# Layer B with token-major keys and heads innermost, query features of three chunks held at once, masks in halves, and the first loads reordered: a scheduled two-layer attention kernel

## The chip, the cores and the metric

The kernel runs on one core of one Trainium2 chip. The metric is device time in microseconds (us) of that core for one execution. The kernel before took 632.72 us (median of 3 runs, 631.79 to 635.19). Five engines matter: PE (matrix multiplies; PEld is its weight load, which overlaps it), ACT (activation functions, copies), DVE (vector work), POOL (masks, small work) and SP (issues transfers). Runs come with a state, fast or slow. Every comparison below is between fast runs.

## The reference, cut to what matters

Two different attention layers, A and B, alternate, twice: A, B, A, B, each with a layer norm ahead and a residual sum. There are 2048 tokens, 512 features, 32 heads of 16.

```python
def _A_ref(x, wq, wk, wv, wo, beta):      # causal softmax inside 4 segments of 512 tokens, plus a
    ...                                   # memory M, z carried from one segment to the next
        logits = einsum('bhqd,bhkd->bhqk', qs, ks) * scale + mask
        a_dot = einsum('bhqk,bhkd->bhqd', softmax(logits), vs)
        a_mem = (pq @ M) / (pq @ z + 1e-06)
        o = g * a_mem + (1.0 - g) * a_dot
        M = M + einsum('bhld,bhle->bhde', phi(ks), vs)
    ...
def _B_ref(x, wqkv, w_phi, wo):           # linear attention over all 2048 tokens
    ...
    phi_k = concatenate([softmax(pk), softmax(-pk)])   # pk = k @ w_phi, softmax over a head's 16
    kv = einsum('bhsf,bhsd->bhfd', phi_k, v)           # needs the keys of every token
    z = einsum('bhsf->bhf', phi_k)
    num = einsum('bhqf,bhfd->bhqd', phi_q, kv)
    den = einsum('bhqf,bhf->bhq', phi_q, z)[..., None] + 1e-06
    return (num / den) ... @ wo
```

One thing shapes the whole time line: a query of B needs `kv` and `z`, sums over all tokens. B's keys and values can follow A segment by segment, but no query product of B can start before A's last segment has passed through B's keys. Each layer pair therefore ends in a stretch of query work alone; after the second pair, nothing else is left to run beside it.

## The kernel before

The program is a graph of operations. A list scheduler with estimated durations orders them on each engine at build time, giving each operation its tiles from pools; a class of tiles may have a cap on how many are alive.

```python
LAT = {"pe": 190, "act": 160, "dve": 130, "pool": 100, "sp": 60}
...
                while ready[e]:                       # forward(): the pick on each engine
                    pr, i = heapq.heappop(ready[e])
                    o = ops[i]
                    if o.eng is not None:
                        continue
                    if can_alloc(o):                  # a free tile, and the class under its cap
                        pick = o
                        break
                    skipped.append((pr, i))
...
        self.pD = Pool("pD", dbl, psum=True)          # 2 PSUM tiles D, 128x1024 f32
        self.pG = Pool("pG", sgl, psum=True)          # 4 PSUM tiles G, 128x512 f32
...
N_XT, N_Q4, N_K1, N_K2, N_VT, N_SM, N_KT = 5, 7, 28, 14, 5, 6, 6
CAP2 = {"EQ": 6, "ET": 4}      # EQ: a 128x1024 block of query features, 4 for each chunk of 512 tokens
TOK = {3: ((0, 1, 2), (3,))}   # only chunk 3 has token-major keys
```

A's attention makes scores (S) in a D tile, an exp of 1024 columns on ACT, and on the diagonal a mask on POOL:

```python
self.mm(... KT.t[:, hf, j * 128:(j + 1) * 128], Q4.t[:, :, i * 128:(i + 1) * 128] ..., opens=[PT], label="S")
self.act(lambda PT=PT: PT.t[:], lambda S=S: S.t[:], ACT.Exp, 1024, [S], [PT], scale=0.25, label="exp")
if j == i:
    v(lambda e, pt8=pt8: e.affine_select(pt8(), pt8(), [[0, 8], [1, 128]], ...), 1080, [PT], [PT], eng="pool", label="mask")
```

B's keys of chunks 0 to 2 are feature-major: logits in D tiles, exps of 1024 columns, normalisers by small matmuls (Zk), then DMA transposes to token-major for the KV product:

```python
def b_keys(self, L, c):
    for gp in range(2):
        S = self.T(self.pD, "S")                      # the same two D tiles as A's scores
        ... # 8 BK matmuls of 512 columns
        for sgn in range(2):
            self.act(... ACT.Exp, 1024, [S[0], S[512]], [ET[sgn]], scale=1.0 - 2.0 * sgn, label="kexp")
            self.mm(... [8] * 8, [ET[sgn], R("H8b")], [Zb[(gp, sgn)]], label="Zk")
            for gg in range(2):
                self.tr(... , label="Etr")            # DMA transpose
    ... # reciprocal of Zk, BV matmuls, values times reciprocal, KV matmuls
```

B's queries: 16 BQ matmuls a chunk, exps into EQ, normalisers Zq, a serial scaling on ACT and DVE, and then for each of 4 token tiles a product N, a multiply on DVE straight from PSUM, an output projection:

```python
def b_query(self, L, c, store):
    ...
        self.wproj(S, gg * 512, self.WB["q"], ..., opens=[EQ[(gp, 0)], EQ[(gp, 1)]], label="BQ")
        self.act(... ACT.Exp, 1024, [S[0], S[512]], [EQ[(gp, sgn)]], label="qexp")
    ... # Zq, then Ln, Exp, five small DVE steps, Ln, Exp
    for tt in range(4):
        N = self.T(self.pD, "S")
        ...
        v(lambda e, ...: e.tensor_tensor(Tm.t[:].rearrange("p (s h d) -> p s h d", s=2, h=H),
                                         N.t[:].rearrange("p (s h d) -> p s h d", s=2, h=H),
                                         ab()[:, tt, :, :, None].to_broadcast([128, 2, H, DH]), ALU.mult), 1131, ..., label="nmul")
```

The softmax here doesn't subtract the row's maximum and nothing guards it: scores larger than these inputs give would overflow.

## Time and profile before

The stretches are cut at A's scores: their first and last matmul in each of the two layer pairs. This is the view of busy time by window, kernel before. After the window and its length come the busy time of each engine in it (with instructions), the granted PE clock as a share of full, the DMA share and GB/s.

```profile
core 0: us, PE busy (x) PEld busy (x) DVE busy (x) ACT busy (x) POOL busy (x), PEclk, DMA share, GB/s
0.00:27.70 27.70, 9.64 (x40) 4.02 (x41) 22.86 (x56) 12.07 (x21) 19.18 (x33) 0.98 0.58 184
27.70:248.90 221.20, 202.33 (x2289) 114.00 (x2320) 172.24 (x348) 190.08 (x223) 94.04 (x121) 0.98 0.33 63
248.90:318.20 69.30, 55.52 (x511) 33.12 (x518) 48.31 (x103) 37.16 (x59) 8.33 (x19) 0.87 0.10 22
318.20:546.60 228.40, 207.31 (x2316) 115.26 (x2348) 171.59 (x344) 194.81 (x231) 87.91 (x109) 0.98 0.32 56
546.60:632.80 86.20, 60.58 (x534) 34.98 (x539) 46.27 (x84) 32.79 (x53) 1.88 (x3) 0.84 0.19 47
```

The five lines are start-up, scores of the first pair, the query work between, scores of the second pair, and the tail. In the score stretches PE is about 91% busy. In the tail PE has 61 of 86 us, DVE 46, ACT 33: no engine is full, and the clock has dropped to 0.84.

Three lines of the page, kernel before: busy time with its share of the span, and PE's busy share and granted clock in tenths over 40 equal slices.

```profile
PE 535.4 (85%) x5680; PEld 301.4 (48%) x5760; DVE 461.3 (73%) x932; ACT 466.9 (74%) x586; POOL 211.3 (33%) x285
...
PE   1688998999999898679898888999989999958775
...
PEclk9889999999999999859989899999989999976897
```

The row of the clock shows two dents, at the ends of the two score stretches: there PE was busy for only 5 to 8 tenths of a slice.

The waits, kernel before: what ACT waited for at L514 over the whole span (us in total, times, longest). L514 is the helper of all exps, so the line holds key and query exps too, and the longest wait, 8.1 us, is a query exp of the tail shown below. The same view for the two score stretches alone gives 22.7 and 24.1 us.

```profile
ACT p L514 <- PE D L508: 73.2, 92, 8.1
```

Groups of instructions by line and shape, kernel before: busy us and mean ns, then idle time before them and its causes. They are the query multiply, the layer norm's last step xn, and a bf16 add.

```profile
L1086 DVE TENSOR_TENSOR p<-D,pS 128x1024 bf16<-128x1024 f32 x32 | 38.0, 1215 | 1.9 <-PE D L508 1.7
...
L754 DVE TENSOR_SCALAR p<-X,mv,rstd 128x512 bf16<-128x512 bf16 x48 | 32.9, 688 | 16.0 <-POOL rstd L743 15.4
...
L782 DVE TENSOR_TENSOR p<-p 128x512 bf16<-128x512 bf16 x48 | 27.1, 567 | 0.3
```

Last, the timeline of the tail, kernel before, between two multiplies of L1086: start, busy us, engine, line, operation (count), and in brackets the idle time before it.

```profile
592.17 2.35 DVE L1086 TENSOR_TENSOR p<-D,pS 128x1024 bf16<-128x1024 f32 x2
...
593.85 4.80 PE L508 MATMUL D<-pX,WB_q 128*128 128x512 bf16 x15 [1.58 <-DVE p L1086]
...
596.96 2.99 ACT L514 ACTIVATE p<-D 128x1024 bf16<-128x1024 f32 x3 [8.09 <-PE D L508]
...
599.77 0.35 PE L508 MATMUL G<-Rz,p 128*128 128x16 bf16 x8
...
600.62 1.03 ACT L514 ACTIVATE p<-D 128x1024 bf16<-128x1024 f32 x1
...
603.27 0.64 ACT L514 ACTIVATE pS<-pS 128x128 f32<-128x128 f32 x2
...
604.27 2.35 DVE L1086 TENSOR_TENSOR p<-D,pS 128x1024 bf16<-128x1024 f32 x2
```

These lines follow one chunk change from top to bottom. PE projects the next chunk's queries (4.80 us), ACT makes the features, the last of them at 600.62 and 1.03 us long, Zq matmuls run, Ln and Exp scale, and only at 604.27 does the next multiply start. With a cap of 6 on EQ tiles and 4 to a chunk, the next chunk's last features can't be made before this chunk has given its own back.

### The profile page before, as it was taken

The page shows a single profiled execution, that of the slowest core. Times are in us where ns is not written, and L with a number is a line of the kernel's source. Part 1 is how long each engine was busy: PE and PEld are TensorE (multiplying, and loading weights), DVE is VectorE, ACT ScalarE, POOL GpSimd, SP SyncE. Part 2 cuts the span into 40 slices and gives each one's busy share as a digit, 9 for nine tenths or more (in the row PEclk, how much of TensorE's full clock was granted, in tenths as well). Part 3 has the DMA queues.
Part 4 walks back from the last instruction along what each step waited for, and adds up shares of the span by engine and source line. Part 5 has one row for each costly group of instructions (what it writes and reads, how often), then busy time and mean ns, then how long its engine had stood idle before and what let it go on. Part 6 is the DMA issues. An engine that isn't in the chain of part 4 may idle for free.

```text
span 632.8 us, 13820 instructions
## 1 busy us (share of the span) xinstructions
PE 535.4 (85%) x5680; PEld 301.4 (48%) x5760; DVE 461.3 (73%) x932; ACT 466.9 (74%) x586; POOL 211.3 (33%) x285
## 2 busy tenths in 40 slices
PE   1688998999999898679898888999989999958775
PEld 0344544555556455355444444456445555526342
DVE  8789888688686585567779847778948758755563
ACT  4468999899889898427768789898969889733442
POOL 8483426225335432002223435433523533200000
PEclk9889999999999999859989899999989999976897
DMA  3872423421241241000353222352133133001232
GB/s 100 267 137 63 78 52 51 82 46 40 54 75 21 43 76 19 2 1 8 75 88 79 55 35 66 60 77 44 43 62 65 19 52 67 11 0 34 60 84 75
DMA packets 110511, 37.38 MB, mean 59 GB/s; under 512 B 101584, under 2 KB 109296, under 8 KB 110448
## 3 DMA queue, kind: packets, MB, share of 16 engines
q1 hardware_dynamic: 109088, 31.75, 26.3%
q0 software_dynamic: 1360, 4.74, 2.3%
q8 instruction: 45, 0.74, 0.5%
q14 instruction: 18, 0.15, 0.1%
HBM read 6.32 MB, written 2.10 MB: 13 GB/s over the span
## 4 chain that ended last, share of the span: by engine, by line
PE 42%; DVE 34%; ACT 9%; POOL 6%; DMA 5%; issue 3%; SPq 0%; POOLq 0%
PE G L508 24%; PE D L508 16%; ACT p L514 7%; DVE p L1086 3%; DMA p<-p 3%; DVE stats L738 3%; DVE pK L522 3%; DVE p L754 3%; DVE p L782 3%; POOL rstd L743 2%; DVE X L933 2%; DVE p L776 2%; POOL p L873 1%; DVE p L893 1%; DVE p L522 1%
## 5 line engine op out<-in xcount | busy, mean ns | idle before, releaser
L514 ACT ACTIVATE p<-D 128x1024 bf16<-128x1024 f32 x376 | 366.9, 1030 | 75.6 <-PE D L508 73.2
L873 POOL TENSOR_SCALAR_AFFINE_SELECT p<-p 128x1024 bf16<-128x1024 bf16 x128 | 141.7, 1112 | 190.1 <-ACT p L514 189.3
L508 PE MATMUL D<-pQ,pK 128*128 128x512 bf16 x640 | 181.8, 382 | 13.6 <-ACT p L514 6.7
L508 PEld LDWEIGHTS G<-pV,p 128*128 128x128 bf16 x2656 | 85.1, 96 | 33.5 <-POOL p L873 8.1
L508 PE MATMUL G<-pV,p 128*128 128x17 bf16 (+1 forms) x2656 | 89.4, 173 | 6.3 <-POOL p L873 2.6
L508 PEld LDWEIGHTS D<-pQ,pK 128*128 128x128 bf16 x640 | 49.7, 97 | 71.3 <-ACT p L514 32.2
L741 POOL TENSOR_SCALAR rstd<-mv 128x1 f32<-128x1 f32 x64 | 15.6, 246 | 151.8 <-DVE mv L739 151.2
L933 DVE TENSOR_TENSOR X<-X,G 128x512 bf16<-128x512 bf16 x32 | 21.9, 684 | 35.4 <-PE G L508 35.3
L738 DVE BATCH_NORM_STATS2 stats<-X 128x6 f32<-128x512 bf16 x64 | 43.1, 681 | 5.6 <-ACT X L521 4.9
L963 DVE TENSOR_TENSOR pT<-G,pT 128x1024 bf16<-128x1024 f32 x32 | 38.7, 1216 | 10.5 <-PE G L508 10.0
L514 ACT ACTIVATE p<-G 128x512 bf16<-128x512 f32 x64 | 38.8, 607 | 8.6 <-PE G L508 4.1
L754 DVE TENSOR_SCALAR p<-X,mv,rstd 128x512 bf16<-128x512 bf16 x48 | 32.9, 688 | 16.0 <-POOL rstd L743 15.4
L522 DVE CAST pK<-G 64x512 bf16<-64x512 f32 x52 | 35.5, 684 | 6.0 <-PE G L508 5.3
L1086 DVE TENSOR_TENSOR p<-D,pS 128x1024 bf16<-128x1024 f32 x32 | 38.0, 1215 | 1.9 <-PE D L508 1.7
L508 PE MATMUL G<-pX,WA_q 128*128 128x512 bf16 x120 | 33.5, 403 | 6.7 <-DVE MS L841 2.6
L743 POOL TENSOR_TENSOR rstd<-rstd,mhalf 128x1 f32<-128x1 f32 x64 | 37.8, 594 | 4.1
L508 PE MATMUL G<-WB_v,pX 128*128 128x512 bf16 x114 | 31.5, 396 | 7.6 <-DVE pT L548 5.3
L508 PE MATMUL G<-WB_o,p 128*128 128x512 bf16 x126 | 35.7, 408 | 1.6 <-ACT p L514 0.7
L508 PE MATMUL G<-WA_v,pX 128*128 128x512 bf16 x119 | 32.4, 402 | 3.1 <-DVE nb L748 1.2
L508 PE MATMUL G<-pX,WA_k 128*128 128x512 bf16 x118 | 32.0, 390 | 2.3 <-DVE MS L839 1.2
L508 PE MATMUL D<-pX,WB_q 128*128 128x512 bf16 x122 | 31.2, 393 | 3.2 <-DVE p L1086 3.0
L548 DVE RECIPROCAL pS<-G 128x32 f32<-128x32 f32 (+1 forms) x64 | 20.5, 323 | 17.8 <-PE G L508 17.5
(120 smaller groups left out, 737.0 us busy)
## 6 DMA issues: line engine op xcount, KB each, us to landing
pQ<-p SPq DMA_DIRECT2D x128, 32.0 KB, 1.8
p<-p SPq DMA_TRANSPOSE x128, 2.5
out_dram<-X SPq DMA_DIRECT2D x16, 128.0 KB, 1.7
X<-in_A_x_dram POOLq DMA_DIRECT2D x3, 512.0 KB, 8.4
pX<-in_B_wqkv_dram POOLq DMA_DIRECT2D x2, 512.0 KB, 6.9
pX<-p SPq DMA_TRANSPOSE x54, 2.5
X<-in_A_x_dram SPq DMA_DIRECT2D x4, 128.0 KB, 2.9
pX<-in_A_wq_dram SPq DMA_DIRECT2D x1, 512.0 KB, 4.8
```

The source lines that it names most:

```text
L508: ins = e.matmul(out_ap, lhsT, rhs, start=st, stop=sp, tile_position=(basep(lhsT), basep(out_ap)))
L514: return self.g.op({"act": (dur, lambda e: e.activation(out_ap(), in_ap(), func, scale=scale))}, reads, writes, opens, label=label)
L522: "dve": (n / 0.96 + 65, lambda e: e.tensor_copy(out_ap(), in_ap()))}
L548: return e.reciprocal(o, i)
L738: v(lambda e: e.bn_stats(self.stats[:, t, :], self.X[:, t, :]), 602, [R("X", t)], [R("st", t)], label="bn")
L743: v(lambda e: e.tensor_tensor(rs, rs, self.mhalf[:], ALU.pow), 120, [R("rstd", t), R("mhalf")], [R("rstd", t)], eng="pool", label="rstd")
L754: v(lambda e: e.tensor_scalar(xn.t[:], self.X[:, t, :], self.mv[:, t, 0:1], self.rstd[:, t:t + 1], op0=ALU.subtract, op1=ALU.mult), 300, [ ...
L782: v(lambda e: e.tensor_tensor(dst.t[:], dst.t[:], e_.t[:], ALU.add), 335, [dst, e_], [dst], label="phadd")
L873: v(lambda e, pt8=pt8: e.affine_select(pt8(), pt8(), [[0, 8], [1, 128]], ALU.is_ge, 0.0, base=0, channel_multiplier=-1), 1080, [PT], [PT], ...
L933: self.v(lambda e: e.tensor_tensor(self.X[:, t, :], self.X[:, t, :], ps.t[:, 0:512], ALU.add), 602, [R("X", t), ps[0]], [R("X", t)], label ...
L963: self.v(lambda e: e.tensor_tensor(Vt.t[:, :, :, 0:16], ps.t[:, None, 0:512].to_broadcast([128, 2, 512]).rearrange("p s (h d) -> p s h d", ...
L1086: v(lambda e, tt=tt, N=N, Tm=Tm: e.tensor_tensor(Tm.t[:].rearrange("p (s h d) -> p s h d", s=2, h=H), N.t[:].rearrange("p (s h d) -> p s h ...
```

## The change

Its intent is to hide work in the query stretches and to relieve engines in the score stretches. It is a bundle of parts, cut here to the core.

```diff
 # 1. keys of every chunk token-major (old b_keys is gone, b_keys_tok becomes b_keys)
-TOK = {3: ((0, 1, 2), (3,))}
+TOK = {0: ((0, 1, 2, 3),), 1: ((0, 1, 2, 3),), 2: ((0, 1, 2, 3),), 3: ((0, 1, 2), (3,))}
 # 2. (dim, head) order of B's values, KV and outputs: heads innermost; the product copied on ACT first
-            v(lambda e, ...: e.tensor_tensor(Tm.t[:].rearrange("p (s h d) -> p s h d", s=2, h=H), N.t[:]...,
-                              ab()[:, tt, :, :, None].to_broadcast([128, 2, H, DH]), ALU.mult), 1131, ...)
+            w = lambda tt=tt: ab()[:, tt, :, :].rearrange("p s (g h) -> p (s g) h", h=8)[:, :, None, :].to_broadcast([128, 2 * NG, 16, 8])
+            if (L, t) in COPIED:                      # all 32 tiles; ab is bf16 now
+                self.act(... Ns.t[:], ... N.t[:], ACT.Copy, 1024, [N], [Ns], label="Nev")
+                v(... e.tensor_tensor(shape(Tm.t[:]), shape(Ns.t[:]), w(), ALU.mult), 600, ..., port=True)
 # 3. query features of three chunks
-N_XT, N_Q4, N_K1, N_K2, N_VT, N_SM, N_KT = 5, 7, 28, 14, 5, 6, 6
-CAP2 = {"EQ": 6, "ET": 4}
+N_XT, N_Q4, N_K1, N_K2, N_VT, N_SM, N_KT = 5, 6, 22, 19, 5, 6, 6
+CAP2 = {"EQ": 12, "ET": 6}
 # 4. masks in halves
-          v(lambda e, pt8=pt8: e.affine_select(pt8(), ..., [[0, 8], [1, 128]], ...), 1080, [PT], [PT], eng="pool", label="mask")
+          for hh in range(2):
+            v(lambda e, pt4=pt4: e.affine_select(pt4(), ..., [[0, 4], [1, 128]], ...), 560, [PT], [PT[hh]], eng="pool", label="mask")
 # 5. scheduler: a marked DVE operation is not started while POOL is busy in the model; new transpose figures
-                    if can_alloc(o):
+                    if e == "dve" and o.port and free["pool"] > now + 1e-9:
+                        held = True
+                    elif can_alloc(o):
-        return self.g.op({"sp": (1180.0, ... transpose=True)])}, ..., lat=1450.0, ...)
+        return self.g.op({"sp": (1310.0, ... transpose=True)])}, ..., lat=1320.0, ...)
 # 6. start-up: all large loads on SP, weights in halves, later ones gated by early layer norms;
 #    rstd of four tiles on ACT; Q4 zero-fills spread over DVE, ACT, POOL; first segment's Q4 by masks, not DMA
-        ldx(4, 4, "pool")
+        ldx(4, 4)
+        if root == "act":
+            ... activation(rs, self.mv[:, t, 1:2], ACT.Ln, bias=self.epsln[:, 0:1])
+            ... activation(rs, rs, ACT.Exp, scale=-0.5)
+MASKED = {(0, 0)}
... (about 450 more lines: layouts, resources, permuted weights)
```

## The prediction

> **What bounds it now.** The page: PE busy 85% of 632.8 us, ACT 74%, DVE 73%. By stretch (busy time by window): start-up 0-64 us (PE 40, DVE 55 of 64); attention 64-258 and 358-555.5 (PE 182 of 196, ACT 170: PE-bound, ACT close); a gap after each attention, 258-276.5 and 555.5-573.8 (PE 10 of 18, ACT 5, granted clock 0.70); first queries with the next projections 276.5-358 (PE 70, DVE 67 of 81.5); last queries 573.8-632.8 (PE 42, DVE 30, ACT 22 of 59: nothing full). There the chain of waits goes four times, 15 us apart, through small DVE/ACT steps, N matmuls, the 1.22 us DVE multiply reading PSUM, and BQ projections (3.5 to 4.8 us).
>
> **What changes.**
> 1. Keys token-major. Out: 192 Zk matmuls (about 30 ns apart, 6 us of PE), 48 of 182 DMA transposes. In: 48 Zred reductions (0.684 us: +33 us DVE), 48 exps of 512 columns for 24 of 1024 (0.607 against 1.03 us: +4.4 us ACT).
> 2. Head-inner layout: ACT copies the query product N (32 x 1.03 = +33 us), DVE multiplies in bf16 from SBUF. The 512-column bf16 adds take 0.41 us, so I estimate 0.65 for 1024, against 1.215: -18 us DVE. The Trainium skill, "Vector Engine (DVE) Microarchitecture Reference" section 5.1, wants all operands two bytes wide with inner step 1 for two results per cycle; heads innermost gives that, the old broadcast did not. No run shows it yet.
> 3. EQ cap 6 to 12: the program order has 48 instead of 20-24 BQ matmuls ahead of the first query product. They fall into the idle gap. About 24 matmuls (5 to 9 us) leave each query stretch, and PE stays warm.
> 4. Masks 2 x 512 instead of 1 x 1024 (1.11 us). DVE operations lengthen beside a mask (bf16 add 0.41 to 1.25 us, xn 0.41 to 1.16); by mean over shortest about 34 us are lost so. Halves should return about 15.
> 5. Start-up: rstd of four tiles on ACT, no POOL memset ahead of it (3.5 us of the chain), masks instead of the 7.1 us DMA wait before the first scores, later loads gated.
>
> Total work does not fall (DVE level, ACT +45 us, PE -6). The gain is in stretches where nothing is full.
>
> **Sum.** Start-up -6; each attention -3 (PE and mask contention less, ACT and Zred more); gaps -1 each; first queries -8; last queries -13 (16 tiles at about 2 us of PE or ACT, one BQ, 9 us drain: 46 for 59). About -35, shaded to -31 for schedule noise: **602 us, 8 in 10 between 588 and 617**. Faster by over 2%: 0.92; within 2%: 0.07; slower: 0.01.
>
> **What would show it.** First S matmul near 15-18 us instead of 27.7. In the gaps PE above 15 of 18 us, clock near 1. Last stretch 43 to 50 us, its multiply near 0.65. Attention 188 to 198 us each, DVE there 5 to 10 us busier; bf16 add and xn means 0.1 to 0.2 us shorter.
>
> **What would make it wrong.** ACT: 45 us more beside 87% busy attention could lengthen it 5 us each. BQ ahead of the last key block could delay it (PE runs in order). Broadcast bf16 operands may miss double rate (multiply 1.1 us, last stretch gains only 6). DMA transposes on one queue (1.3 us to issue) could bound the tail. More gain if the start-up keeps all 12 us.

## More of the kernel before

Now the second score stretch's chain of waits, kernel before: the share of the stretch that each engine and line has in the chain that ended last.

```profile
by line: PE G L508 24.1%; PE D L508 19.0%; ACT p L514 9.3%; DVE stats L738 4.2%; DVE pK L522 4.0%; DVE p L782 3.7%; issue 3.1%; DVE p L776 2.9%; DMA p<-p 2.9%; DVE X L933 2.3%; DVE p L1086 1.9%; DVE p L893 1.9%; DVE p L903 1.8%; POOL rstd L
```

PE has 43% of it, but the DVE lines listed add up to over 22%.

## The result and the profile after

The changed kernel took **562.75 us** (median of 4 runs, 560.82 to 565.80); the kernel before took 633.42 in all its runs up to then (median of 4). The ratio is 0.8888, with a 95% interval from 0.8836 to 0.8941. A ratio here and below is the mean time of one kernel's fast runs over that of the other's of the same rounds, so it is not quite the ratio of the medians quoted. The output was correct. The prediction's range, 588 to 617, missed: the kernel gained 70 us where 31 were predicted.

The same windows, kernel after, cut at the same events; columns as before.

```profile
core 0: us, PE busy (x) PEld busy (x) DVE busy (x) ACT busy (x) POOL busy (x), PEclk, DMA share, GB/s
0.00:17.60 17.60, 6.83 (x32) 3.30 (x32) 13.53 (x43) 15.43 (x27) 5.55 (x16) 1.00 0.59 179
17.60:230.80 213.20, 197.27 (x2235) 108.27 (x2236) 176.59 (x389) 199.56 (x252) 99.92 (x180) 1.00 0.26 57
230.80:289.50 58.70, 55.44 (x514) 33.30 (x513) 47.54 (x114) 49.91 (x77) 9.66 (x20) 0.97 0.11 23
289.50:498.90 209.40, 200.61 (x2277) 111.28 (x2276) 169.88 (x367) 193.97 (x243) 96.95 (x172) 1.00 0.22 47
498.90:559.30 60.40, 52.20 (x513) 30.28 (x511) 36.24 (x86) 46.05 (x69) 2.01 (x4) 1.00 0.25 66
```

| stretch | before, us | after, us | difference | predicted |
|---|---|---|---|---|
| to the first score | 27.7 | 17.6 | -10.1 | -6 |
| scores, first pair | 221.2 | 213.2 | -8.0 | -3 |
| between (gap, first queries) | 69.3 | 58.7 | -10.6 | -9 |
| scores, second pair | 228.4 | 209.4 | -19.0 | -3 |
| tail (gap, last queries) | 86.2 | 60.4 | -25.8 | -14 |
| span | 632.8 | 559.3 | -73.5 | -35, shaded to -31 |

The prediction cut its stretches a little differently, so the last column is its terms laid beside the nearest stretch. Two terms carry the miss: the score stretches, -27.0 together for -6, and the tail. (How the gain falls on the first and the second score stretch moves with the order alone, as the neutral edits below show; only the sum is to be read.)

The same lines of the page, kernel after:

```profile
PE 512.3 (92%) x5568; PEld 286.4 (51%) x5568; DVE 443.8 (79%) x995; ACT 504.9 (90%) x664; POOL 214.1 (38%) x392
...
PE   2768998999999999998998999899999999999797
...
PEclk9999999999999999998999999999999999999999
```

ACT has 38 us more work, as the change asks of it, and the time still fell by 70. PE's busy time fell by 23 us. The 192 Zk matmuls are gone: the weight loads fall from 5760 to 5568, while the matmul records fall by only 112 because the trace before lacks 80 of them. The dents of the clock row are gone too, and the same work takes less time at the higher clock: a matmul of B's output projection took 408 ns on average before and 379 after.

The second score stretch's chain of waits, kernel after:

```profile
by line: PE G L516 43.3%; PE D L516 21.2%; ACT p L522 13.4%; DMA p<-p 4.0%; DMA pX<-p 3.9%; DVE pK L531 2.7%; issue 1.3%; DVE pT L1010 1.2%; POOL p L907 1.2%; DVE p L808 0.7%; DVE X L967 0.7%; DVE pS L1028 0.6%; SPq L846 0.6%; DVE p L927 0.
```

The DVE lines shown went from over 22% to about 6%, and PE from 43% to 64%. PE was busy for 207.3 of 228.4 us before and for 200.6 of 209.4 after, so its idle time fell from 21.1 to 8.8 us and its busy time by 6.7. The shares of the chain are a weaker sign: in n2 (below), the same work in another order, the stretch took 208.8 us as well, with 45% for the PE lines shown and 33% for ACT's exps and copies.

The same waits, kernel after (L522 is now the helper of exps and of the copies of N):

```profile
ACT p L522 <- PE D L516: 24.7, 52, 2.4
```

That is 49 us less of waiting for D tiles over the whole span. In the two score stretches it is 8.5 and 7.0 us, 31 us less; the other 17 us or so are waits for query logits and products. The groups, kernel after:

```profile
L1102 DVE TENSOR_TENSOR p<-p,pS 128x1024 bf16<-128x1024 bf16 x32 | 21.6, 699 | 0.1
L814 DVE TENSOR_TENSOR p<-p 128x512 bf16<-128x512 bf16 x48 | 21.6, 452 | 0.4
L785 DVE TENSOR_SCALAR p<-X,mv,rstd 128x512 bf16<-128x512 bf16 x48 | 20.4, 435 | 4.5 <-POOL rstd L774 4.1
```

The multiply takes 0.699 us for 1.215; the xn step and the add lose less time. The timeline of the tail's multiplies, kernel after:

```profile
524.46 1.29 DVE L1102 TENSOR_TENSOR p<-p,pS 128x1024 bf16<-128x1024 bf16 x2
...
526.00 0.68 DVE L1102 TENSOR_TENSOR p<-p,pS 128x1024 bf16<-128x1024 bf16 x1
...
527.54 0.68 DVE L1102 TENSOR_TENSOR p<-p,pS 128x1024 bf16<-128x1024 bf16 x1
...
530.90 1.29 DVE L1102 TENSOR_TENSOR p<-p,pS 128x1024 bf16<-128x1024 bf16 x2
...
532.79 0.68 DVE L1102 TENSOR_TENSOR p<-p,pS 128x1024 bf16<-128x1024 bf16 x1
...
539.86 0.68 DVE L1102 TENSOR_TENSOR p<-p,pS 128x1024 bf16<-128x1024 bf16 x1
```

At a chunk change before, no multiply ran for 9.2, 9.75 and 7.9 us (from the end of a pair such as 592.17 + 2.35 to the next at 604.27): 26.9 us in all. After, only two holes over 2 us are left: 2.7 us (528.22 to 530.90) and 6.4 us (533.47 to 539.86). From the first multiply's start to the last one's end it was 49.0 us before and 25.1 after.

### The profile page after: what moved, and what is told of

Same layout as the page of the kernel before. It is cut to its first block, busy times and chain, and to the rows that moved or that the text cites. A ratio compares the mean times of both kernels' runs of the same rounds, so it can differ in the third digit from the quotient of the medians.

```text
span 559.3 us, 13738 instructions
## 1 busy us (share of the span) xinstructions
PE 512.3 (92%) x5568; PEld 286.4 (51%) x5568; DVE 443.8 (79%) x995; ACT 504.9 (90%) x664; POOL 214.1 (38%) x392
## 4 chain that ended last, share of the span: by engine, by line
PE 62%; ACT 17%; DVE 10%; DMA 7%; issue 2%; SPq 1%; POOL 1%
PE G L516 40%; PE D L516 22%; ACT p L522 14%; DMA p<-p 4%; DMA pX<-p 1%; DVE pK L531 1%; DVE stats L764 1%; DMA wphi_st<-in_B_w_phi_dram 1%; DMA X<-in_A_x_dram 1%; ACT pQ L851 1%; DVE KV L982 1%; DVE p L810 0%; DVE Rkv L986 0%; DVE pT L1010 0%; POOL p L907 0%
## 5 line engine op out<-in xcount | busy, mean ns | idle before, releaser
L522 ACT ACTIVATE p<-D 128x1024 bf16<-128x1024 f32 x384 | 378.0, 1044 | 26.3 <-PE D L516 24.7
L907 POOL TENSOR_SCALAR_AFFINE_SELECT p<-p 128x512 bf16<-128x512 bf16 x256 | 161.0, 654 | 185.1 <-ACT p L522 184.6
L516 PEld LDWEIGHTS D<-pQ,pK 128*128 128x128 bf16 x640 | 50.6, 97 | 69.3 <-ACT p L522 32.1
L522 ACT ACTIVATE p<-G 128x512 bf16<-128x512 f32 x112 | 69.3, 629 | 7.9 <-PE G L516 7.3
L1028 DVE TENSOR_REDUCE pS<-p 128x32 f32<-128x512 bf16 x64 | 42.9, 678 | 20.4 <-ACT p L522 20.0
L1010 DVE TENSOR_TENSOR pT<-G,pT 128x1024 bf16<-128x1024 f32 x30 | 36.2, 1210 | 6.0 <-PE G L516 5.8
L557 DVE RECIPROCAL pS<-G 128x32 f32<-128x32 f32 (+1 forms) x64 | 20.3, 321 | 22.1 <-PE G L516 21.5
L531 DVE CAST pK<-G 64x512 bf16<-64x512 f32 x46 | 31.5, 684 | 7.3 <-PE G L516 5.7
L516 PE MATMUL G<-WA_o,p 128*128 128x512 bf16 x128 | 32.9, 379 | 4.2 <-DMA p<-p 3.1
L774 POOL TENSOR_TENSOR rstd<-rstd,mhalf 128x1 f32<-128x1 f32 x60 | 34.4, 578 | 3.3
L516 PE MATMUL G<-WB_k,pX 128*128 128x512 bf16 x128 | 32.7, 379 | 1.4 <-DVE X L967 0.8
L516 PE MATMUL G<-WB_o,p 128*128 128x512 bf16 x128 | 32.8, 379 | 0.0
```

Source lines behind the costliest of these rows:

```text
L516: ins = e.matmul(out_ap, lhsT, rhs, start=st, stop=sp, tile_position=(basep(lhsT), basep(out_ap)))
L522: return self.g.op({"act": (dur, lambda e: e.activation(out_ap(), in_ap(), func, scale=scale))}, reads, writes, opens, label=label)
L531: "dve": ((340 if fast else n / 0.96 + 65), lambda e: e.tensor_copy(out_ap(), in_ap()))}
L557: return e.reciprocal(o, i)
L774: v(lambda e: e.tensor_tensor(rs, rs, self.mhalf[:], ALU.pow), 540, [R("rstd", t), R("mhalf")], [R("rstd", t)], eng="pool", label="rstd")
L907: v(lambda e, pt4=pt4: e.affine_select(pt4(), pt4(), [[0, 4], [1, 128]], ALU.is_ge, 0.0, base=0, channel_multiplier=-1), 560, [PT], [PT[hh ...
```

## The experiments

Eighteen kernels ran, all with three timed rounds, in five groups on five occasions. The parts of the change were undone one at a time (names a and b), then disputed costs inside the largest parts were taken away (c, d), the scheduler's luck was measured (n, c4), and two parts were put alone into the kernel before (f). Unless said otherwise an edit is against the kernel after, and "stretch" is as in the table above, read from each run's own profile to within 0.4 us (0.8 for the scores of both pairs). In those sessions the kernel before had medians from 632.96 to 635.31 us.

I began with this theory: the extra gain is less POOL contention on DVE in the score stretches and a tail where the serial chain of a chunk change is hidden. The rival: the gain in the score stretches is from token-major keys, or is luck of the schedule.

### How much is luck? Four neutral edits

```diff
# c4_tr_model: the scheduler's old figures for a DMA transpose, nothing else
-{"sp": (1310.0, ...)}, lat=1320.0
+{"sp": (1180.0, ...)}, lat=1450.0
# n1_lat_pe: one latency of the model
-LAT = {"pe": 190, "act": 160, ...}
+LAT = {"pe": 200, "act": 160, ...}
# n2_lat_act
+LAT = {"pe": 190, "act": 170, ...}
# n3_before_tr: the new transpose figures, in the kernel before
```

> The changed kernel with the scheduler's old figures for a DMA transpose (issue 1.18, landing 1.45 us instead of 1.31 and 1.32). It changes no instruction's work, only the order. It measures how much a neutral reordering moves the time: if under 3 us (560 to 566), single edits that moved more than that mean something; if 5 us or more, the single edits of 7 to 9 us are not told from scheduling luck.

> The changed kernel with only the scheduler's figure for a wait on PE at 200 instead of 190 ns: no work changes, only the order. Luck small: 560 to 566. Luck large, as the run with the old transpose figures says (569.9): anywhere from 556 to 572.

> The changed kernel with only the scheduler's figure for a wait on ACT at 170 instead of 160 ns. As for the other neutral order: 560 to 566 if luck is small, 556 to 572 if it is large. If all three neutral orders lie above 565, the submitted order is a lucky one and some 4 to 7 of the 70 us are its luck.

> The kernel before with only the new figures for a DMA transpose (1.31 and 1.32 us instead of 1.18 and 1.45). If these figures are truer and help: 622 to 630. If it is luck: 628 to 642.

| run | median, us (range) | ratio (95%) | first score | scores, both | between | tail |
|---|---|---|---|---|---|---|
| after | 562.75 (560.82 to 565.80) | 0.8888 (0.8836 to 0.8941) | 17.6 | 422.4 | 58.7 | 60.6 |
| c4 | 569.92 | 0.8998 (0.8972 to 0.9025) | 17.3 | 435.7 | 54.5 | 60.2 |
| n1 | 559.69 (559.32 to 561.39) | 0.8832 (0.8806 to 0.8858) | 18.6 | 421.3 | 56.3 | 61.0 |
| n2 | 565.04 | 0.8908 (0.8877 to 0.8939) | 18.1 | 425.2 | 56.1 | 63.6 |
| n3 (of before) | 638.01 | 1.0045 (1.0009 to 1.0081) | 25.6 | 452.1 | 67.2 | 87.6 |

These edits change no work, only the order and, where the scheduler may choose, the engine of a copy (in c4 DVE has 11 instructions more and ACT 11 fewer). The four orders of the same work run from 559.7 to 569.9 us, and the scores of both pairs from 421.3 to 435.7. This is the ruler for everything below: a single edit that moves the total by less than about 7 us, or the scores within those bounds, is not told from luck; and four orders are few, the true spread may be wider. The orders also move time between the two score stretches: 210.7 to 221.5 us for the first, 208.7 to 214.8 for the second. The new transpose figures are no part of the gain in before (638.01, a little slower). The order n1 is the fastest version seen, but its interval overlaps that of the change, and I don't call it better.

### The masks and the port rule

```diff
# a1_mask_whole: one mask of 1024 columns again
-   for hh in range(2): v(... [[0, 4], [1, 128]] ..., 560, [PT], [PT[hh]], eng="pool", label="mask")
+   v(... [[0, 8], [1, 128]] ..., 1080, [PT], [PT], eng="pool", label="mask")
# a2_no_hold: the scheduler's port rule off
-   if e == "dve" and o.port and free["pool"] > now + 1e-9:
+   if False:
# b1_whole_nohold: both
```

> The changed kernel with the mask as one 128x1024 operation again, everything else kept. Theory P (the shared port between DVE and POOL cost the attention its time, halves freed it): attention of 64-230 and 312-499 us grows by 3 to 6 us each, means of xn back from 0.435 to 0.55 us or more, DVE above 10% of the chain in attention instead of about 3%; in all +6 to +12 us on 562.75 (ratio to before 0.898 to 0.908). Rival O (the scheduler's new order did it, masks do not matter): within 3 us of 562.75 (ratio 0.884 to 0.894).

> The changed kernel with the scheduler's new rule switched off (a DVE operation marked as port user is held back while POOL is busy in its model), masks still in halves. Theory O (order): +6 to +12 us (ratio 0.898 to 0.908), chain of attention full of DVE again. Theory P (halves alone suffice): at most +4 us (ratio below 0.895); xn mean up to 0.5 us at most.

> The changed kernel with both undone: mask as one operation and the scheduler's port rule off. Each alone cost nothing (562.9 and 563.5 us). Theory P2 (either one keeps DVE and POOL apart, so only both undone bring the old contention back): xn mean above 0.6 us, 128x512 bf16 add above 0.53, DVE busy +15 us or more, attention +3 to +6 us each, in all +6 to +14 us (569 to 577; ratio 0.898 to 0.911). Rival (with PE and ACT as the limits of attention, DVE time lost to the port is hidden): DVE means rise as said but the time stays within 3 us.

Alone, neither does anything: 562.90 us (0.8873) with whole masks, 563.51 us (0.8878) without the rule. The mean of xn is 0.447 and 0.513 us in them, of the add 0.440 and 0.461, against 0.435 and 0.452 in the kernel after. Both undone together bring 571.64 us (0.8988, 0.8960 to 0.9016). The groups of b1, as shown for the kernel after:

```profile
L814 DVE TENSOR_TENSOR p<-p 128x512 bf16<-128x512 bf16 x48 | 29.1, 607 | 0.6 <-ACT p L811 0.2
L785 DVE TENSOR_SCALAR p<-X,mv,rstd 128x512 bf16<-128x512 bf16 x48 | 27.2, 571 | 7.0 <-POOL rstd L774 5.2 <-DMA p<-p 1.2 <-ACT rstd L770 0.4
```

So the contention is real. By their starts and ends in the trace of b1, the 17 adds of L814 that overlap a mask took 0.965 us on average, the 31 others 0.411. The add is longer than in the kernel before (0.567), xn makes up about half of its way back to 0.688, and DVE's busy time is 467.1 us for 443.8. Either remedy is enough for the time, and 23 us of lost DVE time came with 9 us of the total, an amount at the edge of the ruler (its scores, 433.0 us, lie inside it). My first theory for the score stretches fell here.

One more reading of b1, from the pages: the chain of waits over the whole span by engine, before, after and b1.

```profile
PE 42%; DVE 34%; ACT 9%; POOL 6%; DMA 5%; issue 3%; SPq 0%; POOLq 0%
PE 62%; ACT 17%; DVE 10%; DMA 7%; issue 2%; SPq 1%; POOL 1%
DVE 35%; PE 34%; ACT 16%; DMA 9%; issue 3%; POOL 3%; SPq 0%; DVEq 0%; ACTq 0%
```

b1 has as much DVE in its chain as the kernel before, yet its score stretches are 17 us shorter (433.0 against 449.6). DVE's share of the chain alone does not say how long they get.

### The cap on query features, and its buffers

```diff
# a3_eq6
-CAP2 = {"EQ": 12, "ET": 6}
+CAP2 = {"EQ": 6, "ET": 6}
# b5_k2_14_eq6: the same, and 14 buffers as before (with 12 EQ in 14 buffers the scheduler gets stuck)
-N_XT, N_Q4, N_K1, N_K2, ... = 5, 6, 22, 19, ...
+N_XT, N_Q4, N_K1, N_K2, ... = 5, 6, 22, 14, ...
```

> The changed kernel with the cap of EQ tiles back from 12 to 6, so one and a half chunks of query features ahead instead of three. Theory G (the gain after the attention is BQ work moved into the gap before the first query product): gap idle again (PE 12 to 13 of 18 us), query stretches +5 to +9 us each, in all +10 to +18 us (ratio 0.905 to 0.917). Rival C (the ACT copy of N and the fast multiply made the query stretches short): within 4 us of 562.75.

> The changed kernel with EQ cap 6 and 14 instead of 19 of the 2 KB buffers that PT, ET, EQ and T share (12 EQ tiles do not fit in 14: the scheduler gets stuck, so both go together). EQ 6 with 19 buffers took 578.5 us. Theory B (more PT buffers let ACT run ahead in attention): attention +4 to +8 us each against that run, 586 to 595 us. Rival (PT is never short, D tiles in PSUM are): within 3 us of 578.5.

a3 took 578.47 us (0.9123, 0.9062 to 0.9184): 15.7 us more by the medians. The scores stayed (421.7), the tail grew by 10.0, the stretch between by 6.6. The first score also came 3.8 us later than in the kernel after. The same shift (3.5 to 3.9 us) is in b5 and in a4 below, though none of these edits touches the start-up; I count it as order and not as the cap. The holes are back where they were in the kernel before; the timeline of DVE, a3:

```profile
537.22 0.68 DVE L1102 TENSOR_TENSOR p<-p,pS 128x1024 bf16<-128x1024 bf16 x1
...
544.45 1.29 DVE L1102 TENSOR_TENSOR p<-p,pS 128x1024 bf16<-128x1024 bf16 x2
...
546.33 1.28 DVE L1102 TENSOR_TENSOR p<-p,pS 128x1024 bf16<-128x1024 bf16 x2
...
556.23 1.29 DVE L1102 TENSOR_TENSOR p<-p,pS 128x1024 bf16<-128x1024 bf16 x2
```

No multiply runs from 537.90 to 544.45, from 547.61 to 556.23, and once more for 8.3 us: 23.4 us in three holes, although each multiply is short now. The holes belong to the cap, not to the multiply. b5 took 583.26 us (0.9179); the 4.8 us more than a3 are under the ruler.

### The same cap in the kernel before

```diff
# f1_before_eq12, against the kernel before
-N_XT, N_Q4, N_K1, N_K2, N_VT, N_SM, N_KT = 5, 7, 28, 14, 5, 6, 6
-CAP2 = {"EQ": 6, "ET": 4}
+N_XT, N_Q4, N_K1, N_K2, N_VT, N_SM, N_KT = 5, 6, 22, 19, 5, 6, 6
+CAP2 = {"EQ": 12, "ET": 6}
```

> The kernel before with only the EQ cap of 12 and the buffers it needs (19 of the 2 KB tiles, 22 of the 1 KB ones, 6 query tiles, ET cap 6). If the part adds as its removal subtracted (15.5 us, and about 5 for the buffers): 612 to 622. If in the kernel before the last queries hang on the DVE multiply and the order, so that BQ moved ahead is not the limit: 626 to 636.

It took 609.11 us (607.31 to 611.26; ratio 0.9625, 0.9594 to 0.9656). Two lines of constants (the EQ cap, the pool sizes of the change, and ET's cap) give 24 us of the 70: the tail fell from 86.2 to 66.6 us, the stretch between by 4.1, the scores by 1. The window of its tail, columns as above:

```profile
540.80:607.40 66.60, 56.20 (x538) 33.60 (x544) 43.78 (x81) 35.75 (x56) 1.88 (x3) 0.92 0.26 60
```

First to last multiply went from 49.0 to 32.0 us, with the multiplies themselves unchanged at 1.22 us. This part stands alone, and it is larger than the whole of what I had predicted for the last queries.

### The copy on ACT, and heads innermost

```diff
# a4_direct: DVE multiplies straight from PSUM
-COPIED = {(L, t) for L in range(2) for t in range(16)}
+COPIED = set()
# c3_head_outer: copied as after, but the multiply's broadcast is innermost (step 0); a wrong
# result on purpose, to cost the access pattern alone
-w = ... [:, :, None, :].to_broadcast([128, 2 * NG, 16, 8])
+w = ... [:, :, None].to_broadcast([128, 2 * H, DH])
```

> The changed kernel without the ACT copy of N: DVE multiplies from PSUM again (1.21 us for 0.70 plus 1.03 of ACT), layout and EQ cap kept. Theory C: last stretch 6 to 10 us longer, first queries 3 to 6 longer, in all +9 to +16 us (ratio 0.903 to 0.914). Theory G: within 4 us, since DVE is not full in the last stretch (25 of 42 us) and ACT loses 33 us of work.

> The changed kernel with the multiply's broadcast as the old layout would have it: the weight repeated along the innermost dimension (step 0) instead of heads innermost (step 1); wrong result on purpose. If the double rate needs inner step 1 on every operand: the multiply takes 1.10 to 1.25 us instead of 0.70, DVE +13 to +17 us, time +2 to +6 us (565 to 569; the run without the copy took 569.9). If step 0 is as good: multiply 0.70, time unchanged within 2 us, and the layout change was not needed for it.

a4 took 569.91 us (0.8984, 0.8926 to 0.9041), its multiply 1.216 us; its tail grew by 3.5 us and its first score came 3.9 us later. The 7 us are at the edge of the ruler. c3 took 576.16 us (0.9086). Its group, as above:

```profile
L1102 DVE TENSOR_TENSOR p<-p,pS 128x1024 bf16<-128x1024 bf16 x32 | 38.7, 1233 | 0.1
```

All operands are two bytes wide in SBUF in both, and of the steps only the innermost of one operand differs (the rows are also cut into 16 elements instead of 16 by 8): 0.699 us against 1.233. With this layout the copy bought nothing; at 1.233 us the multiply is as slow as from PSUM, the copy comes on top, and the tail is 70.0 us. (c3's wrong result still passed the comparison with the reference, presumably because the weights differ little from head to head. It must not be used.)

### The start-up

```diff
# b3_old_start: old loads (large ones on the POOL queue), rstd on POOL, old zero-fills
-        ldx(4, 4)
+        ldx(4, 4, "pool")
-MASKED = {(0, 0)}
+MASKED = set()
... (the other loads, the memsets and rstd likewise)
```

> The changed kernel with the old start-up: loads as before (16 of them issued from POOL), rstd of the first tiles on POOL, POOL or DVE memsets of the query tiles, the first segment's query tiles filled by DMA. Theory S (the start-up's 10 us lead at the first score matmul is kept to the end): first S at 26 to 29 us, in all +9 to +13 us (572 to 576). Rival (the lead is eaten by later waits): at most +5 us.

It took 575.64 us (0.9065, 0.9043 to 0.9087), 12.9 more by the medians. The first score came at 30.2 us for 17.6, 12.6 us later, and no later stretch was far from the kernel after (423.7, 56.6, 63.1). The chain of waits up to its first score, by line:

```profile
by line: DMA pQ<-p 20.5%; DVE pK L704 10.8%; DVE pQ L709 9.1%; DVE Rz L714 7.7%; DVE stats L756 7.6%; DVE p L777 7.4%; issue 7.3%; PE G L549 6.3%; PE G L516 6.2%; SPq L838 6.1%; ACT p L530 2.0%; PE D L516 1.9%; DVE GAm L682 1.9%; DVE pX L53
```

The transfer that spreads the first queries (20.5% of 30.2 us, 6.2 us) and the zero-fills (pK, pQ) lead it. The lead at the start is kept to the end: what is saved there is saved whole.

### Feature-major keys again

```diff
# b2_feature_keys: the old key routine for chunks 0 to 2, in the new value layout
-                self.b_keys(L, s, TOK[s])
+                self.b_keys(L, s, TOK[s]) if s == 3 else self.b_keys_feat(L, s)
# c1_feat_no_tr, against b2: no DMA transposes; the KV matmuls read the untransposed features (wrong on purpose)
-                    self.tr(..., label="Etr")
# c2_feat_no_zk, against b2: 24 matmuls in place of the 192 Zk (wrong on purpose)
-                self.mm(... [8] * 8, [ET[sgn], R("H8b")], [Zb[(gp, sgn)]], label="Zk")
+                self.mm(... [64], [ET[sgn]], [Zb[(gp, sgn)]], label="Zk")
# d1_feat_g, against b2: logits in G tiles, exps of 512 columns, the rest feature-major as in b2
-            S = self.T(self.pD, "S")
+                S = self.T(self.pG, "gen")
-                self.act(... ACT.Exp, 1024, [S[0], S[512]], [ET[sgn]], ...)
+                    self.act(... ACT.Exp, 512, [S[0]], [ET[sgn][gg]], ...)
```

> The changed kernel with feature-major keys again for chunks 0 to 2 (1024-column exps, 192 Zk matmuls, 48 DMA transposes of E, no Zred there), new head-inner layout kept. Theory K (token-major keys gave the attention its speed, by freeing the DMA transpose queue and PE, and because one key tile needs only one chunk quarter): attention +5 to +10 us each, in all +10 to +20 us (573 to 583). Rival: the swap is work-neutral (DVE -33, PE +6, ACT -4 us): within 4 us.

> The run with feature-major keys (581.6 us), without its 48 DMA transposes of E: the KV products read the untransposed tile, so the result is wrong on purpose and every shape is kept. Theory T (the transposes, about 1.3 us each to issue and 2.4 to land on one queue, are what feature-major keys cost): 12 to 18 us faster, 564 to 570. Rival D (the cost is the blocks of 16 BK matmuls and four 1024-column exps that take the two D tiles from the scores): within 4 us of 581.6.

> The run with feature-major keys (581.6 us), with 4 matmuls of 64 columns per chunk in place of the 32 Zk matmuls of 8 (24 against 192 in all; wrong result on purpose, same waits). Theory Z (PE time of Zk): about 30 ns each for 168 matmuls, 5 us faster, 576 to 578. Rival T or D: within 2 us of 581.6.

> The run with feature-major keys (581.6 us), its key logits written to four G tiles per chunk with 512-column exps instead of two D tiles with 1024-column exps; transposes and Zk kept. Rival D (D tiles taken from the scores are the cost): 10 us or more faster, 566 to 572. If it stays within 5 us of 581.6, D falls too and what remains is the whole chunk's lockstep (all four key quarters must be there before any KV product).

| run | median, us | ratio (95%) | scores, both |
|---|---|---|---|
| b2 | 581.63 | 0.9155 (0.9136 to 0.9175) | 441.3 |
| c1, no transposes | 581.17 | 0.9174 (0.9147 to 0.9201) | 436.5 |
| c2, hardly any Zk | 578.02 | 0.9122 (0.9090 to 0.9154) | 435.7 |
| d1, logits in G | 569.50 | 0.8974 (0.8952 to 0.8997) | 426.9 |

b2 costs 18.9 us, all of it in the scores (441.3 for 422.4, outside the ruler). Neither the transposes (c1: nothing) nor the Zk matmuls (c2: 3.6 us) are the reason. (c1 keeps the untransposed tiles in use until the KV products, which could cost something of its own.) Where the logits lie is, for the larger part: d1 gets 12 of the 19 us back. It also cuts the exps in halves, so that finer steps are not separated from the place. The other 7 us stay unexplained. The waits over the whole span, b2 and then d1:

```profile
ACT p L522 <- PE D L516: 41.0, 66, 2.8
```

```profile
ACT p L522 <- PE D L516: 26.5, 53, 2.7
```

In the kernel after it was 24.7 us. In the two score stretches alone it is 26.8 us in b2, 15.6 in d1 and 15.5 in the kernel after: the 11 us between b2 and d1 match the 12 us of the time. Feature-major logits take the two D tiles that scores need, each for eight matmuls and two exps of 1.03 us; in that time the exps of scores wait.

### Logits in G tiles, in the kernel before

```diff
# f2_before_feat_g, against the kernel before: the edit of d1
```

> The kernel before with only the key logits of chunks 0 to 2 written to G tiles with 512-column exps, the rest feature-major as it was. If D tiles taken from the scores cost the attention there too: 6 to 14 us faster, 620 to 628. If the attention of the kernel before is held by DVE (a quarter of its chain there): within 5 us of 634.

If the two D tiles were the whole story, this should have made the kernel before faster. Its three fast runs took 635.15 to 641.44 us (ratio 1.0078, 1.0030 to 1.0126); the fourth, the profiled one (644.71), gives no stretches. It gained nothing. So in the kernel before something else must have held the score stretches. I took it for the DVE work in their chain, but that is argued and not shown, and b1 speaks against DVE's share alone. Token-major keys as a whole, put alone into the kernel before, were not run.

## Why the prediction was wrong

**The last queries: the step that failed first.** The prediction put "last queries -13", as "16 tiles at about 2 us of PE or ACT, one BQ, 9 us drain: 46 for 59". Its mechanism was right: in the kernel after, 48 of the 64 BQ matmuls of the last chunks run between the last score and the first multiply and 16 later; before, 22 were recorded there. The drain was right too: 9.7 us from the last multiply to the end. The term that failed is the tiles with the one BQ, about 37 us by the prediction and 25.1 measured. It priced a tile at 2 us of engine time. The time line of the kernel before says otherwise: of the 49.0 us from first to last multiply, 26.9 are the three holes of the chunk changes, in which the whole chain ran in series (BQ, exps, Zq, Ln and Exp, small DVE steps, the first product), so 16 tiles took 22.1 us, 1.4 each. Another 23.4 us of holes are in a3 with the short multiply. The term should have been those holes, read from the time line. Measured: from first multiply to the end, 59.0 us before (573.8 to 632.8) and 34.8 after (524.5 to 559.3), -24.2 for -13. f1 shows that the cap, with its buffers, gives 20 of the tail's 26 us with no faster multiply; a3 shows that the cap alone takes 10 of the 26 away again. The gain was off by nearly a factor of two. The Trainium skill's "Perfetto Trace Analysis", section Optimization Strategy, advises interleaving regimes where the most-contended engine changes, and says that consistent bubbles can mean too few buffers for the next tile; this case agrees (three bubbles of 8 to 10 us in the kernel before, 24 us gained by f1's buffers and cap).

**The score stretches: the second step that failed.** The prediction put "each attention -3", from "PE-bound, ACT close". Measured: -8.0 and -19.0. What was wrong is that PE left little to gain: PE stood idle for 40.0 of the 449.6 us of both stretches, and ACT waited 46.8 us for D tiles in them. After, PE was idle for 24.7 us (15.3 less) and busy for 397.9 us (11.8 less, from 409.6; Zk is gone and the clock is higher, and I did not split the two), and ACT's wait was 15.5 us. Most of it is the token-major keys (b2, 18.9 us), through the D tiles (d1, 12 us of them, with waits from 41.0 to 26.5 us). The 8 us beyond the keys are within the ruler. But f2 shows that moving the logits is no gain in the kernel before, so it depends on the rest of the change. Which part of the rest makes room for it I did not separate: the exact share of masks and port rule, copy, cap and keys in these 27 us stays open.

**Contention on DVE.** Right in kind, and of little weight in the total. The prediction expected halves to return "about 15" us of DVE time; xn went from 0.688 to 0.435 us and the add from 0.567 to 0.452, together 18 us of busy time. The Trainium skill's "SBUF — State Buffer", section Who interferes with whom, says that a DVE instruction with two SBUF inputs contends with a POOL instruction that reads SBUF; the adds of b1 agree, 0.965 us beside a mask and 0.411 without one. But b1 puts the whole of it at about 9 us of the total, at the edge of the ruler, and a1 shows that the halves are not needed beside the scheduler's rule.

**The gaps.** Right. Between the last score and the first multiply PE had 18.72 of 27.2 us before, at a clock of 0.79, and 22.77 of 25.6 us after, at 1.00. These are the windows, before and then after, with the columns of the tables above:

```profile
546.60:573.80 27.20, 18.72 (x213) 11.50 (x211) 16.68 (x37) 11.25 (x16) 1.88 (x3) 0.79 0.00 1
```

```profile
498.90:524.50 25.60, 22.77 (x249) 13.66 (x247) 15.50 (x38) 20.12 (x27) 2.01 (x4) 1.00 0.01 1
```

The gap itself shortened by 1.6 us for a predicted 1, and this is not told from luck: the three neutral orders have 25.4 to 28.3 us. The clock agrees with the Trainium skill's "TensorE: Matmul & The Clock Gate", Part 1, What's actually happening: the throttled state is the default and activity releases it. In before's gap four BV matmuls took 1.03 us at 551.58, and four more took 1.89 at 564.25, after 2.64 us without work; in after's gap both groups took 1.03.

**The multiply.** Right: 0.699 us, estimated at 0.65. The Trainium skill's "Vector Engine (DVE) Microarchitecture Reference", section 5.1, asks for two-byte operands and an innermost step of one on all of them for two results per cycle; c3 broke the step and got 1.233 us. Its worth to the total is small: a4, which has neither copy nor fast multiply, is 7 us slower, at the edge of the ruler.

**The start-up.** Right in mechanism, too careful in size: -10.1 for -6. "More gain if the start-up keeps all 12 us" was among the reasons for being wrong, and b3 shows just that, 12.9 us.

**The first queries.** Right: with the gap -9 predicted, -10.6 measured.

**Total work.** "DVE level, ACT +45 us, PE -6": DVE fell by 17 us, ACT rose by 38, PE's busy time fell by 23. Not every part of the first was traced. The last should be the clock (0.949 to 0.997 over the span) and the Zk matmuls (some 6 us by the prediction's own estimate); their shares were not measured. The fear that "45 us more beside 87% busy attention" would lengthen the score stretches did not come true, at 90% ACT over the span.

**The shading.** I shaded the sum by 4 us "for schedule noise". The neutral orders spread over 10 us, so a range of 29 us around a sum of small terms left little for two terms that are wrong by 11 and 21 us.

The undoings add up to about the gain (12.9 start, 18.9 keys, 15.7 cap, 4.8 buffers, 7.2 copy, 8.9 contention: 68 of 70 us), but with a ruler of 7 us for each, a start-up shift of 4 us inside two of them and an interaction shown by f2 this is a rough agreement and no proof of a split.

## What to carry to other kernels

Cost a buffer cap by the hole that it leaves on the time line, from the last use before it to the first use after it, and not by the busy time of the engine whose work will move. Before calling a stretch bound by its busiest engine, price that engine's idle time and see what releases it: 91% busy still left 40 us in two stretches, and 15 of them went. The chain of waits shows where to look, but its shares move with the order and are no measure of the time. Where a scheduler orders the program, run a few edits that change nothing but the order first; their spread, 10 us here from four orders, is a first measure of the smallest effect that one edit can show.

## What the Trainium skill lacked or had wrong

- None of the pages that I used says what an order alone is worth. Four orders of the same work on one core took 559.69 to 569.92 us; a page on measuring (it would belong to "Perfetto Trace Analysis") should say that one run of one order is no ruler.
- "Perfetto Trace Analysis", section Identifying the Most-Contended Engine, says to optimize first the engine with the highest occupancy, and for TensorE to judge by the busy share of its weight loads (or by FLOPs) and not of its matmuls. By that, ACT (74%) came first before the change, then DVE (73%), and PE's weight loads had 48%. Here ACT was given 38 us more work (to 90% of the span) while the time fell by 70 us. Occupancy over a span did not find the 26.9 us of serial holes; the line on consistent bubbles in the next section points at them.
- "SBUF — State Buffer", section Who interferes with whom, agrees with the traces on the contention of a two-input add (0.965 us beside a mask, 0.411 without), but has no measure of what the lost time costs a kernel: 23 us of DVE busy time came with about 9 us here.
- No page that I used has the cost of splitting a POOL mask: 128 of 1024 columns took 1.112 us each, 256 halves 0.654 us each, 141.7 against 161.0 us in all.
